# Later score products, spread-out norms and another queue for one copy, in a fused channel-attention and gated feed-forward kernel

## The chip, the cores and the metric

The kernel runs on one core of a Trainium2 chip. The metric is device time in microseconds, as the median of several runs. A core has four engines that compute and run side by side: TensorE (PE, matrix products into the PSUM memory), VectorE (DVE), ScalarE (ACT) and GpSimd (POOL). SyncE (SP) only issues transfers; GpSimd and ScalarE can issue them too. Each engine takes its instructions in program order, and semaphores make it wait for the others.

## The reference, cut to what matters

Four batches of 6016 rows and 256 channels. A channel attention makes a 256 x 256 matrix per batch from q and k, and a gated feed-forward layer follows.

```python
B, N, C = (4, 6016, 256)
qn = q / (np.linalg.norm(q, axis=1, keepdims=True) + 1e-06)
kn = k / (np.linalg.norm(k, axis=1, keepdims=True) + 1e-06)
s = kn.transpose(0, 2, 1) @ qn / tau
s = s - s.max(-1, keepdims=True)
a = np.exp(s)
a /= a.sum(-1, keepdims=True) + 1e-09
x = (v @ a).reshape(B * N, C)                       # 24064 x 256
gate = 1.0 / (1.0 + np.exp(-(x @ w_gate)))          # 256 x 1536
val = x @ w_val
out = gate * val @ w_out                            # 1536 x 256
```

## The kernel before

The kernel folds the attention matrix into the two input weights of the layer (`gh_G`, `gh_H`), so that the main loop runs on v alone. The loop goes over 4 batches, 12 chunks of 512 rows in each, and 12 blocks f of 128 hidden columns in each chunk: 144 turns per batch. Such a turn is called a slot here. In each slot TensorE makes a gate and a value tile, ScalarE the gate's function, VectorE their product hT, and TensorE about 7 output products of an earlier chunk (which are saved by a Strassen-like scheme of 7 products in place of 8, with sums of operands made on VectorE):

```python
def glu(b, ci, f, between=None):
    ...
    for ps, w in ((ps_gate, G), (ps_val, H)):
        for ib in range(CB):
            mm(ps[:, :n], w[...], vT[:, ib, :nt, :], start=(ib == 0), stop=(ib == CB - 1))
    ...
    nc.scalar.activation(out=g_sb[:, :n], in_=ps_gate[:, :n], func=ACT.Tanh, scale=0.5)
    nc.vector.scalar_tensor_tensor(out=hts[b, ci][:, f, :n], in0=g_sb[:, :n], scalar=1.0,
                                   in1=ps_val[:, :n], op0=ALU.add, op1=ALU.mult)
```

Beside this, the loop over batch b carries the statistics of batch n = b + 1 as side work, each piece tied to a slot by `at(slot, function, ...)`. Within a slot the order is: `glu`, the output products and their sums, then the side work in the order in which it was listed. q and k come in six groups of 8 row tiles (the last has 7), loaded from GpSimd's queue:

```python
def load_qk(b, t0, nt):
    tl = qkpool.tile([P, 2, 2 * TPC, C], BF16, tag="qk", name="qk_sb")      # 4 buffers
    ...
    for w, src in enumerate((q, k)):
        for u0, r0, n in parts:
            nc.gpsimd.dma_start(out=tl[:, w, u0 : u0 + n, :], in_=rows(src, b)[:, r0 : r0 + n, :])
```

The scores q^T k use 7 products in place of 8, too. Their operand sums qs0 to qs4 are made per group, qs1 by a copy and an accumulating transfer:

```python
def score_sums(b, t0, m, halves):
    ...
    out = qspool.tile([P, 2 * TPC, P], BF16, tag=f"qs{m}", name=f"qs{m}", bufs=1 + (m == 1))
    if m == 0:      # qs0: k's halves, a difference
        tt(out=o[:, :n], in0=tl[:, 1, hi, :], in1=tl[:, 1, lo, :], op=ALU.subtract)
    elif m == 1:    # qs1: q's lower half, copied
        nc.sync.dma_start(out=o[:, :n], in_=tl[:, 0, lo, :])
    ...             # qs2 of q and k, qs3 of q, qs4 of k: nc.vector.tensor_tensor

def score_sum_q(b, t0, halves):     # qs1 += q's upper half
    nc.gpsimd.dma_start(out=o[:, :n], in_=qk[b, t0][:, 0, TPC : TPC + n, :], accum_op=ALU.add)

products = (                        # of score_work; u runs over 4 tiles: 28 products in a full group
    (0, 0, raw(0, 0, 0), split(0, 1), None),        # split(m, .) and block(m, .) read qs<m>
    (0, 1, raw(0, 1, 1), split(0, 0), (...)),
    (1, 0, block(2, 0), block(2, 1), (...)),
    (1, 1, block(3, 1), block(4, 1), (...)),        # index 12 is the first of these
    (1, 2, block(3, 0), block(4, 0), None),
    (0, 2, split(1, 1), raw(1, 0, 0), None),        # index 20
    (0, 3, split(1, 0), raw(1, 1, 1), (...)),
)

def run_scores(lo, hi, slot):
    for _ in range(len(score_queue) // (hi - slot)):
        _, fn, a = score_queue.pop(0)
        fn(*a)
```

The norms: ScalarE squares q and k, GpSimd adds the squares into an accumulator by transfers, VectorE folds it, TensorE sums over the partitions, and GpSimd takes the root in 13 small operations. A row of the result goes through DRAM to all partitions.

```python
def acc_fold(b, w, steps):
    for n in steps:
        nc.vector.tensor_tensor(out=acc[:, :n, :], in0=acc[:, :n, :], in1=acc[:, n : 2 * n, :], op=ALU.add)

def norms_mm(b):                    # four products with a column of ones: two on q, then two on k
    for w in range(2):
        for j in range(CB):
            mm(s["n"][...], s["acc"][w][:, 0, ds(j * P, P)], ones_bf[:, 0:1], ...)
```

The plan of the side work stands in the diff below. In the first batch a group has 13 or 14 slots (80 slots from slot 16 on), in the second and third 16 slots (96 from slot 0 on); the fourth batch prepares nothing.

Of the kernel before, what the change touches and what calls it, by code (L numbers as in the profile page):

```python
# [53 lines left out]
def kernel(  # L54
# [20 lines left out]
    nc = tc.nc  # L75
# [21 lines left out]
    def rows(x, b):  # L97
        return x[b].rearrange("(p t) c -> p t c", p=P)
# [35 lines left out]
    def load_qk(b, t0, nt):  # L134

        tl = qkpool.tile([P, 2, 2 * TPC, C], BF16, tag="qk", name="qk_sb")
        if b and nt < 2 * TPC:

            parts = [(0, t0, nt - TPC), (TPC, t0 + nt - TPC, TPC)]
        else:  # L140
            parts = [(0, t0, nt)]
        for w, src in enumerate((q, k)):
            for u0, r0, n in parts:
                nc.gpsimd.dma_start(out=tl[:, w, u0 : u0 + n, :], in_=rows(src, b)[:, r0 : r0 + n, :])
        if b:
            qk[b, t0] = tl
            return
        for u in range(0, nt, TPC):
            qk[b, t0 + u] = [tl[:, w, u : u + TPC, :] for w in range(2)]
# [10 lines left out]
    t0, nt = groups0[0]  # L160
# [6 lines left out]
    pairs = [(t, 2 * TPC) for t in range(TPC, head - 3 * TPC, 2 * TPC)]  # L167
    loads0 = pairs + [(t, n) for t, n in groups0 if t >= pairs[-1][0] + 2 * TPC]
    load_qk(0, *loads0[0])

    ident_bf = consts.tile([P, P], BF16)
# [20 lines left out]
    for t0, nt in loads0[1:]:  # L192
        load_qk(0, t0, nt)
# [6 lines left out]
    for f0, nf in pieces:  # L200
        if f0 + nf == DFF:
            load_v(0, 1)
        for w, src in enumerate((moe_w_gate, moe_w_val)):
            nc.gpsimd.dma_start(
                out=w_sb[w][f0 // FG][:, :, ds(f0 % FG, nf)],
                in_=src.rearrange("(t p) f -> p t f", p=P)[:, :, ds(f0, nf)],
# [5 lines left out]
    for n in range(FC // TPC):  # L212
        w_f32[n] = f32pool.tile([P, TPC, C], FP32, tag="f32", name="w_f32")
        nc.gpsimd.dma_start(
            out=w_f32[n], in_=moe_w_out.rearrange("(t p) c -> p t c", p=P)[:, n * TPC : (n + 1) * TPC, :]
# [99 lines left out]
    def score_sums(b, t0, m, halves):  # L315
        tl = qk[b, t0]
        s = st[b]
        if m == 0:
            s["sums"] = []
        out = qspool.tile([P, 2 * TPC, P], BF16, tag=f"qs{m}", name=f"qs{m}", bufs=1 + (m == 1))  # L320
        s["sums"].append(out)
        n = halves[0][1]
        lo, hi = (slice(h * TPC, h * TPC + n) for h in range(2))
        tt = nc.vector.tensor_tensor
        if m == 0:

            o = out.rearrange("p (t c) n -> p t c n", c=2).rearrange("p t c n -> p t (c n)")
            tt(out=o[:, :n], in0=tl[:, 1, hi, :], in1=tl[:, 1, lo, :], op=ALU.subtract)
        elif m == 1:

            o = out.rearrange("p (t c) n -> p t c n", c=2).rearrange("p t c n -> p t (c n)")
            nc.sync.dma_start(out=o[:, :n], in_=tl[:, 0, lo, :])
        elif m == 2:

            o = out.rearrange("p (w t) n -> p w t n", w=2)
            tt(out=o[:, :, :n], in0=tl[:, :, lo, :P], in1=tl[:, :, hi, P:], op=ALU.add)
        else:

            w, op = ((0, ALU.subtract), (1, ALU.add))[m - 3]
            for u0, r in [(0, 2 * TPC)] if n == TPC else halves:  # L340
                tt(out=out[:, u0 : u0 + r], in0=tl[:, w, u0 : u0 + r, :P], in1=tl[:, w, u0 : u0 + r, P:], op=op)  # L341
# [494 lines left out]
    for g, (t0, nt) in enumerate(groups0):  # L836
# [11 lines left out]
        while adds:  # L848
            w, last_sq = adds.pop()
# [27 lines left out]
    late = []  # L877
# [27 lines left out]
    def side_work(b):  # L905


        side = {}

        def at(slot, fn, *a):  # L910
            side.setdefault(divmod(slot, FC), []).append((fn, a))

        for ci in range(NCH):
            nb, nci = (b, ci + 1) if ci + 1 < NCH else (b + 1, 0)
            lb, lci = (b, ci + 2) if ci + 2 < NCH else (b + 1, ci + 2 - NCH)
            if nb < B:
                at(ci * FC + 2, transpose_v, nb, nci)
            if lb < B:
                at(ci * FC + (10 if (b, ci) == (0, 0) else 0), load_v, lb, lci)
            if (b, ci) == (0, 0):  # L920
                for i in range(FC // TPC):
                    at(8, copy_w_out, i)
                for n, m in enumerate((1, 0, 3, 2, 4)):
                    for i in range(FC // TPC):
                        at(11 + 2 * n, sum_w_out, m, i)
        n = b + 1
        if n == B:
            return side
        first, last = (16 if b == 0 else 0), 8 * FC
        wide = [(t, min(2 * TPC, NT - t)) for t in range(0, NT, 2 * TPC)]  # L930
        step = (last - first) / len(wide)
        at(first - 1 if b == 0 else 0, acc_start, n)
        for g, (t0, nt) in enumerate(wide):
            s0 = first + int(g * step)
            halves = [(0, nt - TPC), (TPC, TPC)]
            if b == 0:
                at(max(FC - 3, s0 - 14), load_qk, n, t0, nt)
            elif s0 >= 24:
                at(s0 - 24, load_qk, n, t0, nt)
            for i in range(4):  # L940
                at(s0 + 3 * i, acc_square, n, t0, i // 2, halves, i % 2)
            for w in range(2):
                at(s0 + 5 + 6 * w, acc_add, n, t0, w, halves)
            for m, slot in enumerate((0, 0, 3, 6, 9)):
                at(s0 + slot, score_sums, n, t0, m, halves)
            at(s0 + 4, score_sum_q, n, t0, halves)
            at(s0 + 3, queue_scores, n, t0, halves)
            for slot in range(s0 + 3, first + int((g + 1) * step) + 3):
                at(slot, run_scores, s0 + 3, first + int((g + 1) * step) + 3, slot)
        if n + 1 < B:  # L950
            for g, (t0, nt) in enumerate(wide[:2]):
                at(NCH * FC - 24 + 16 * g, load_qk, n + 1, t0, nt)
        s0 = 8 * FC + 2
        at(s0 - 1, acc_fold, n, 0, (4,))
        at(s0, acc_fold, n, 0, (2, 1))
        at(s0 + 1, acc_fold, n, 1, (4,))
        at(s0 + 2, acc_fold, n, 1, (2, 1))
        at(s0 + 3, norms_mm, n)
        at(s0 + 4, root_seed, n)
        at(s0 + 4, root_steps, n)  # L960
        at(s0 + 4, score_out, n, 0)
        at(s0 + 6, score_out, n, 1)
        at(s0 + 7, score_blocks, n)
        at(s0 + 10, norms_inv, n)
        at(s0 + 11, spread_both, n)
        at(s0 + 13, read_row, n)
        at(s0 + 22, scale_x, n, 0)
        at(s0 + 24, scale_x, n, 1)
        at(s0 + 25, exps, n, 0)
        at(s0 + 26, exps, n, 1)  # L970
        at(s0 + 28, all_sums, n)
        at(s0 + 28, gh_tiles, n)
        for i, piece in enumerate(gh_order):
            slot = s0 + 29 + 2 * i
            if slot < NCH * FC:
                at(slot, gh, n, piece, *((pss, "s"), (psm, "m"))[i % 2])
            else:
                spill.setdefault((n, *divmod(slot - NCH * FC, FC)), []).append((gh, (n, piece, psm, "m")))
        return side
# [12 lines left out]
    for b in range(B):  # L992
        side = side_work(b)
        for ci in range(NCH):
            final = (b, ci) == (B - 1, NCH - 1)
            for f in range(FC):
                mid = gh_mid.get(f) if (b, ci) == (0, 0) else None
                glu(b, ci, f, None if mid is None else (lambda: gh_pieces(mid)))
                if prev is not None:
                    if f == 4:  # L1000
                        store()
                    if f + final in NEXT_SLOTS and prev != (0, 0):
                        a_sum(*prev, 1, NEXT_SLOTS[f + final])
                    run_work(work, 1 / max(1, FC - final - f))
                if f in OWN_SLOTS and not final and (b, ci) != (0, 0):
                    a_sum(b, ci, 0, OWN_SLOTS[f])
                for fn, a in spill.get((b, ci, f), []) + side.get((ci, f), []):
                    fn(*a)
                if (b, ci) == (0, 0):
                    gh_pieces(gh_end.get(f, ()))  # L1010
            prev = (b, ci)
            if not final:
                work = out_work(*prev)
# [39 lines left out]
```

## Time and profile before

| | |
|---|---|
| time, median of 3 runs | 818.26 us (817.01 to 819.18) |
| profiled span | 817.8 us |
| VectorE busy | 719.2 us, 88% |
| ScalarE busy | 525.7 us, 64% |
| GpSimd busy | 405.9 us, 50% |
| granted TensorE clock, mean | 0.994 |
| start of slot 0 of the four batches | 36.7, 244.7, 438.4, 632.2 us |
| start of slots 16 and 96 of the first batch | 56.8 and 180.7 us |
| transfers: software queue, hardware queue | 41.4% and 22.2% of 16 engines' span |

The profile gives each engine's busy time, and for each instruction how long its engine stood idle before it and what ended that. "PE ps_s <- DVE qs" is a wait of TensorE, before a product into the tile ps_s, that ended when VectorE had written qs. A line of such a list ends in the sum in us, the number of waits and the longest. In the groups, "L341" is a line of the kernel; most matmuls share line 129, a helper, so one goes by the names of tiles. The granted clock is the share of its full clock that TensorE was given. The slot starts above are read from the timeline, from the gate products.

The transfers by their issuing engine (name, engine, count, KB each, median us from issue to landing):

```profile
qk_sb<-in_q_dram POOLq DMA_DIRECT2D x19, 512.0 KB, 7.9
qk_sb<-in_k_dram POOLq DMA_DIRECT2D x19, 512.0 KB, 10.3
qs<-qk_sb SPq DMA_DIRECT2D x15, 256.0 KB, 6.4
qs<-qk_sb POOLq DMA_DIRECT2D x15, 256.0 KB, 4.0
```

### The profile page before, as it was taken

Reading aid. Unit: us, or ns where it says so; the run is one execution under the profiler, and the core shown is the slowest. Engines: PE = TensorE matmul, PEld = TensorE weight load, DVE = VectorE, ACT = ScalarE, POOL = GpSimd, SP = SyncE. Lnnn points to the kernel's source line nnn. Section 1 sums busy time; section 2 is a strip of 40 time slices with the busy share of each in tenths; the row PEclk is TensorE's granted clock in tenths of the full one; section 3 lists DMA queues with packets and bytes.
Section 4 is the critical chain, followed back from the end, with each engine's and each line's share of the span. In section 5 each row is a group of like instructions: output and inputs, shape, how many; then the busy total and the mean of one; then the engine's idle time right before and its main releaser. Section 6 shows DMA issues by size and latency. Waiting matters only on the chain.

```text
span 817.8 us, 18442 instructions
## 1 busy us (share of the span) xinstructions
PE 782.0 (96%) x6932; PEld 499.8 (61%) x6946; DVE 719.2 (88%) x1234; ACT 525.7 (64%) x893; POOL 405.9 (50%) x622
## 2 busy tenths in 40 slices
PE   3899988899999999999999999999999999999998
PEld 2555655565666666665666666666566566666666
DVE  5778978899988999999998999999998898899896
ACT  3766756665667777775666767766566566656654
POOL 3573544565543555554844355556654234444433
PEclk9999999999999999999999999999999999999999
DMA  9999889772677699865378599976142332432402
GB/s 213 204 195 175 175 166 182 146 134 52 132 140 137 134 187 182 181 131 99 52 136 152 108 181 208 185 140 125 35 104 53 84 66 53 91 65 54 93 30 71
DMA packets 85594, 103.30 MB, mean 126 GB/s; under 512 B 52737, under 2 KB 59521, under 8 KB 85505
## 3 DMA queue, kind: packets, MB, share of 16 engines
q0 software_dynamic: 25840, 59.46, 41.4%
q1 hardware_dynamic: 59088, 41.82, 22.2%
q8 instruction: 54, 0.88, 0.4%
q10 hardware_dynamic: 576, 0.85, 0.3%
q14 instruction: 36, 0.29, 0.1%
HBM read 79.04 MB, written 24.64 MB: 127 GB/s over the span
## 4 chain that ended last, share of the span: by engine, by line
PE 90%; DVE 4%; DMA 4%; issue 1%; ACT 1%; POOL 0%; DVEq 0%; POOLq 0%
PE ps_gate L129 29%; PE ps_val L129 29%; PE ps_o L129 26%; DMA qk_sb<-in_k_dram 4%; PE ps_s L129 4%; PE ps_gh L129 2%; DVE hT L657 1%; DVE sums L679 1%; DVE acc L311 1%; ACT g_sb L656 1%; DVE qs L341 1%; PE ps_end L129 0%; DVE x_sb L518 0%; PE ps_n L129 0%; PE ps_r L129 0%
## 5 line engine op out<-in xcount | busy, mean ns | idle before, releaser
L656 ACT ACTIVATE g_sb<-ps_gate 128x512 f32<-128x512 f32 (+1 forms) x576 | 337.5, 588 | 243.0 <-PE ps_gate L129 231.0
L657 DVE SCALAR_TENSOR_TENSOR hT<-g_sb,ps_val 128x512 bf16<-128x512 f32 (+1 forms) x576 | 386.1, 671 | 80.0 <-ACT g_sb L656 62.3
L129 PE MATMUL ps_gate<-vT,gh_G 128*128 128x512 bf16 (+1 forms) x1152 | 339.2, 376 | 0.4 <-ACT out_sb L764 0.3
L129 PE MATMUL ps_val<-vT,gh_H 128*128 128x512 bf16 (+1 forms) x1152 | 339.0, 376 | 0.0
L679 DVE TENSOR_TENSOR sums<-hT 128x768 bf16<-128x768 bf16 (+1 forms) x460 | 282.7, 615 | 0.0
L129 PEld LDWEIGHTS <-sums 128*128 128x128 bf16 x2670 | 183.7, 98 | 82.5 <-issue 0.8
L129 PEld LDWEIGHTS <-gh_H 128*128 128x128 bf16 x1152 | 112.9, 98 | 131.7 <-issue 2.0
L750 POOL TENSOR_TENSOR out_sb<-out_sb,m_sb 128x256 f32<-128x256 f32 x89 | 79.5, 893 | 206.2 <-ACT out_sb L740 178.0
L129 PE MATMUL ps_o<-w_sums,sums 128*128 128x128 bf16 x1602 | 155.4, 220 | 0.0
L129 PEld LDWEIGHTS <-hT 128*128 128x128 bf16 x1200 | 88.3, 98 | 47.2 <-issue 0.6
L734 POOL TENSOR_TENSOR m_sb<-m_sb 128x128 f32<-128x128 f32 x89 | 44.8, 503 | 138.2 <-ACT m_sb L733 138.0
L129 PEld LDWEIGHTS <-gh_G 128*128 128x128 bf16 x1152 | 90.8, 98 | 11.6 <-DMA vT<-v_sb 0.5
L129 PE MATMUL ps_o<-w_out_sb,sums 128*128 128x128 bf16 x1068 | 96.4, 220 | 0.0
L129 PE MATMUL ps_o<-w_sums,hT 128*128 128x128 bf16 x1068 | 95.8, 220 | 0.0
L751 POOL TENSOR_TENSOR out_sb<-out_sb 128x256 f32<-128x256 f32 x89 | 76.6, 861 | 7.0
L293 ACT ACTIVATE sq<-qk_sb 128x1024 bf16<-128x1024 bf16 (+1 forms) x60 | 61.9, 1031 | 0.0
L740 ACT COPY out_sb<-ps_o 128x512 f32<-128x512 f32 x89 | 52.1, 586 | 11.2 <-PE ps_o L129 8.8
L735 POOL TENSOR_TENSOR m_sb<-m_sb 128x128 f32<-128x128 f32 x89 | 54.4, 611 | 7.0
L733 ACT COPY m_sb<-ps_o 128x384 f32<-128x384 f32 x89 | 42.5, 478 | 3.8 <-PE ps_o L129 1.1
L129 PEld LDWEIGHTS <-qk_sb 128*128 128x128 bf16 x241 | 23.6, 105 | 21.1 <-issue 10.0
L304 POOL DMA_DIRECT2D acc<-sq x36 | 34.9, 1028 | 0.8 <-ACT g_sb L656 0.5
L129 PEld LDWEIGHTS <-qs 128*128 128x128 bf16 x348 | 27.3, 99 | 10.3 <-issue 10.3
(98 smaller groups left out, 462.5 us busy)
## 6 DMA issues: line engine op xcount, KB each, us to landing
out_dram<-out_sb SPq DMA_DIRECT2D x43, 512.0 KB, 3.4
acc<-sq POOLq DMA_DIRECT2D x24, 512.0 KB, 6.9
v_sb<-in_v_dram POOLq DMA_DIRECT2D x44, 256.0 KB, 5.6
qk_sb<-in_q_dram POOLq DMA_DIRECT2D x19, 512.0 KB, 7.9
qk_sb<-in_k_dram POOLq DMA_DIRECT2D x19, 512.0 KB, 10.3
qs<-qk_sb SPq DMA_DIRECT2D x15, 256.0 KB, 6.4
qs<-qk_sb POOLq DMA_DIRECT2D x15, 256.0 KB, 4.0
w_f<-in_moe_w_out_dram POOLq DMA_DIRECT2D x3, 512.0 KB, 9.9
```

The costliest lines, as they stand in the source:

```text
L129: nc.tensor.matmul(out, lhsT=lhsT, rhs=rhs, start=start, stop=stop, **kw)
L293: nc.scalar.activation(out=s["sq", w][:, u0 : u0 + n, :], in_=src[:, u0 : u0 + n, :], func=ACT.Square)
L304: nc.gpsimd.dma_start(out=s["acc"][w][:, u0 : u0 + n, :], in_=s["sq", w][:, u0 : u0 + n, :], accum_op=ALU.add)
L656: nc.scalar.activation(out=g_sb[:, :n], in_=ps_gate[:, :n], func=ACT.Tanh, scale=0.5)
L657: nc.vector.scalar_tensor_tensor(out=hts[b, ci][:, f, :n], in0=g_sb[:, :n], scalar=1.0, in1=ps_val[:, :n], op0=ALU.add, op1=ALU.mult,)
L679: nc.vector.tensor_tensor(out=sums[b, ci, g][:, m, :, : half * P], in0=hT[:, f0 + k0 : f1 : 2, ds(r0 * half * P, half * P)], in1=hT[:, f0 ...
L733: nc.scalar.copy(m, states[p]["ps"][:, : 3 * P].rearrange("p (n c) -> p n c", c=P))
L734: nc.gpsimd.tensor_tensor(out=m[:, 1, :], in0=m[:, 1, :], in1=m[:, 2, :], op=ALU.add)
L735: nc.gpsimd.tensor_tensor(out=m[:, 2, :], in0=m[:, 1, :], in1=m[:, 0, :], op=ALU.add)
L740: nc.scalar.copy(o[:, p : p + half + 1 : half, :], states[p]["ps"].rearrange("p (t c) -> p t c", c=C),)
L750: add(out=ends, in0=ends, in1=states[p]["m"][:, 1:3, :], op=ALU.add)
L751: add(out=ends, in0=ends, in1=mids, op=ALU.subtract)
```

## The change

It moves side work to other slots and changes no arithmetic. In the first batch, the score products of a group begin five slots after the group's start instead of three, and qs4 is made one slot earlier. The squares, folds and loads of k come before those of q. The folds, the norm products, the root and the row are spread over more slots, with the norm products later, and the blocks of the score matrix are put together after the row is sent. The copy of q into qs1 is issued by GpSimd instead of SyncE, one slot later, and the accumulation onto it two slots later. It is meant to give each operand more time between its making and its reading, so that TensorE need not stand for it.

```diff
-        for w, src in enumerate((q, k)):
+        for w, src in ((1, k), (0, q)) if b else ((0, q), (1, k)):
             for u0, r0, n in parts:
                 nc.gpsimd.dma_start(out=tl[:, w, u0 : u0 + n, :], in_=rows(src, b)[:, r0 : r0 + n, :])
 ...
-            nc.sync.dma_start(out=o[:, :n], in_=tl[:, 0, lo, :])
+            nc.gpsimd.dma_start(out=o[:, :n], in_=tl[:, 0, lo, :])
 ...
             for i in range(4):
-                at(s0 + 3 * i, acc_square, n, t0, i // 2, halves, i % 2)
+                at(s0 + 3 * i, acc_square, n, t0, 1 - i // 2, halves, i % 2)
             for w in range(2):
-                at(s0 + 5 + 6 * w, acc_add, n, t0, w, halves)
-            for m, slot in enumerate((0, 0, 3, 6, 9)):
+                at(s0 + 11 - 6 * w, acc_add, n, t0, w, halves)
+            late = 5 if b == 0 else 3
+            for m, slot in enumerate((0, 1, 3, 6, 8 if b == 0 else 9)):
                 at(s0 + slot, score_sums, n, t0, m, halves)
-            at(s0 + 4, score_sum_q, n, t0, halves)
-            at(s0 + 3, queue_scores, n, t0, halves)
-            for slot in range(s0 + 3, first + int((g + 1) * step) + 3):
-                at(slot, run_scores, s0 + 3, first + int((g + 1) * step) + 3, slot)
+            at(s0 + 6, score_sum_q, n, t0, halves)
+            end = first + int((g + 1) * step) + late
+            at(s0 + late, queue_scores, n, t0, halves)
+            for slot in range(s0 + late, end):
+                at(slot, run_scores, s0 + late, end, slot)
 ...
         s0 = 8 * FC + 2
-        at(s0 - 1, acc_fold, n, 0, (4,))
-        at(s0, acc_fold, n, 0, (2, 1))
-        at(s0 + 1, acc_fold, n, 1, (4,))
-        at(s0 + 2, acc_fold, n, 1, (2, 1))
-        at(s0 + 3, norms_mm, n)
-        at(s0 + 4, root_seed, n)
-        at(s0 + 4, root_steps, n)
-        at(s0 + 4, score_out, n, 0)
-        at(s0 + 6, score_out, n, 1)
-        at(s0 + 7, score_blocks, n)
-        at(s0 + 10, norms_inv, n)
-        at(s0 + 11, spread_both, n)
-        at(s0 + 13, read_row, n)
+        at(s0 - 3, acc_fold, n, 1, (4,))
+        at(s0 - 2, acc_fold, n, 1, (2, 1))
+        at(s0 + 1 if b == 0 else s0, acc_fold, n, 0, (4,))
+        at(s0 + 2, acc_fold, n, 0, (2, 1))
+        at(s0 + 5, score_out, n, 0)
+        at(s0 + 6, norms_mm, n)
+        at(s0 + 7, score_out, n, 1)
+        at(s0 + 7, root_seed, n)
+        at(s0 + 7, root_steps, n)
+        at(s0 + 12, norms_inv, n)
+        at(s0 + 12, spread_both, n)
+        at(s0 + 14, read_row, n)
+        at(s0 + 14, score_blocks, n)
         at(s0 + 22, scale_x, n, 0)
```

## The prediction

> **What bounds the kernel now.** I read the page's busy table and its chain first, then the waits of TensorE, then the chain around one wait, then the stretches in a table. A "slot" is one f step of the main loop; batch b of the main loop carries, as side work, the attention statistics of batch b + 1.
>
> ```profile
> PE 782.0 (96%) x6932; PEld 499.8 (61%) x6946; DVE 719.2 (88%) x1234; ACT 525.7 (64%) x893; POOL 405.9 (50%) x622
> PE 90%; DVE 4%; DMA 4%; issue 1%; ACT 1%; POOL 0%; DVEq 0%; POOLq 0%
> ```
>
> TensorE is the bound: 96% busy, 90% of the chain that ended last. A change that touches no matmul can only win back the time in which TensorE stands, or runs at less than its clock. So the question is where it stands. The waits of TensorE after the head (window from 40 us to the end):
>
> ```profile
> PE ps_s L129 <- DVE qs L341: 9.6, 6, 2.2
> PE ps_s L129 <- DVE acc L311: 5.4, 3, 1.8
> PE ps_gate L129 <- ACT out_sb L764: 0.3, 1, 0.3
> ```
>
> Ten waits, 15.3 us, and every large one is in the code that the diff moves. The six on qs all lie between 70 and 177 us, in the loop's first batch; the three on acc come once per batch that prepares another. One of the six, in the chain of waits (start, us, what):
>
> ```profile
> 108.65 0.45 PE ps_gate L129 x2
> 109.10 0.02 issue
> 109.12 0.60 ACT g_sb L656
> 109.73 0.02 issue
> 109.75 0.69 DVE hT L657
> 110.44 0.76 DVE sums L679
> 111.20 0.87 DVE qs L341
> 112.07 0.04 issue
> 112.12 0.27 PE ps_s L129 x2
> ```
>
> This is no overload of VectorE but a loop through three engines: the sum qs4 is put into the same slot (s0+9) as the first product that reads it. VectorE is in order, so qs4 stands behind that slot's hT, which waits for ScalarE, which waits for that slot's gate product. TensorE gets to the end of the slot and must wait for the whole round trip, 2.2 us here.
>
> The stretches (window, PE, PEld, DVE, ACT, POOL busy, granted clock, DMA share, GB/s):
>
> ```profile
> 57.00:181.00 124.00, 114.13 (x1017) 73.44 (x1016) 104.76 (x171) 81.15 (x131) 64.52 (x90) 0.97 0.86 165
> 112.40:115.90 3.50, 3.50 (x16) 1.81 (x15) 1.16 (x2) 0.75 (x2) 0.00 (x0) 0.51 0.63 118
> 181.00:191.00 10.00, 8.19 (x78) 5.19 (x76) 9.04 (x17) 4.81 (x9) 4.48 (x7) 1.00 0.64 133
> 245.00:353.00 108.00, 107.95 (x990) 69.34 (x990) 99.86 (x168) 77.64 (x128) 55.23 (x80) 1.00 0.86 166
> ```
>
> The first stretch is the first batch's score work: TensorE idle for 9.87 of 124 us and the clock at 0.97. The second lies just after the wait above: the clock is 0.51. The fourth is the same work in the second batch, with nothing lost: there a group has 16 slots instead of 13.3, so the product that reads qs4 falls one slot later, and that one slot is enough.
>
> **What the Trainium skill says.** "TensorE: Matmul & The Clock Gate", section "Part 1: The HAM clock gate (the "warmup" mystery)", puts TensorE at half clock after an idle window of about 3.4 us and back at full clock after as long a busy one. The trace agrees on the half and on the way back: after the 2.2 us wait the 128x512 matmuls start about 427 ns apart instead of 216 until 115.9 us, and again near 136 to 139 us. It differs on what it takes: waits of 2.2 us were enough here, though not each time (not after the one that begins near 154.7 us), and after the two shorter ones nothing shows. So a wait can cost more than its own length. "DMA: Bandwidth & Descriptors", section "Queues, rings and completion order", says that each queue keeps its own ring per DMA engine, that descriptors of one ring are taken in order, and that the engine goes round the rings. The trace agrees: a qs accumulation issued by GpSimd at 102.63 us, behind the q and k loads issued at 97.58 and 98.17, landed at 110.02, after k's 108.67. The same page, "Issuing engines are not separate DMA queues", says that another issuing engine saves only issue time. Here the copies on SyncE took 5.2 to 7.5 us to land beside such loads, so the same bytes will not get cheaper by moving; what changes is which line they stand in.
>
> **The change part by part.**
>
> 1. Score products two slots later in the first batch, and qs4 one slot earlier. 28 products of a full group go over 13 or 14 slots, two per slot, so the first reader of qs4 (product index 12) moves from slot s0+9 to s0+5+6 = s0+11, and qs4 from s0+9 to s0+8. The distance goes from 0 to 3 slots, 3 x 1.37 = 4.1 us. The longest wait is 2.2 us, and in the second batch one slot (1.35 us) is enough. All six waits go: 9.9 us of idle time in 57 to 181 us.
> 2. With them the low clock: 0.03 x 124 = 3.7 us. A second count: slot 16 of the first batch starts at 56.8 us and slot 96 at 180.7 us, 123.9 us for 80 slots. The second batch runs at 1.352 us per slot with 165 score products in 96 slots; the same 165 in 80 slots add (2.06 - 1.72) x 56 ns = 0.02 us, so 80 x 1.371 = 109.7 us, and the excess is 14.2 us, of which some 0.5 us is the first chunk's dearer plain output products. 13.6 and 13.7 us agree.
> 3. Norms. The second accumulator's fold now ends at s0-2 (k) and s0+2 (q), and the norm products come at s0+6 instead of s0+3: four slots after the last fold instead of one. The four folds (0.69, 0.75, 0.94 and 1.13 us in the trace) no longer stand in four slots running. 3 x 1.8 = 5.4 us.
> 4. k before q: the same bytes. k's squares, folds and differences come first, so its earlier landing (10.5 us against 7.3 for the one issued first) is what part 3 needs. By itself 0.
> 5. The copy of q from GpSimd: 18 issues of 0.9 us (measured for the qs accumulation), 16 us more on an engine that is 50% busy, not on the path.
>
> Sum: 13.6 + 5.4 = 19.0 us; 818.26 - 19.0 = 799.3 us. I add 1 us for what follows, and predict **800.3 us**.
>
> **Rivals.** *The copy becomes the wait.* SyncE ran far ahead: it issued the fourth group's copy at 107.4 us, 12 us before that group's first slot (119.4). GpSimd goes in step with the loop, and in the first batch the next group's loads stand just ahead in its ring (slots 28, 42, 55, 68 against copies at 30, 43, 57, 70). Landing may take 10 to 12 us from the loads' issue; GpSimd then stands at the accumulation (slot s0+6) for 2 to 4 us, as it does once today (5.8 us), and the sum lands 5 to 8 us later, about slot s0+13 to s0+14. Its first reader (product index 20) is at the end of slot s0+15. By my working 1 to 5 us are left; if it fails in each of five groups by 1 to 2 us, the time is 805 to 809 us. For it speaks that the 16 DMA engines are 86% busy there and the same work will be pressed into 110 us, 97%; against it, that between 280 and 320 us they are as full and nothing waits.
>
> *VectorE becomes the bound of the first batch.* It is busy for 104.8 us there, of some 110 left, 95%. In the second batch it is at 99.9 of 108, 92%, and from 353 to 374 us it is busy for 20.8 of 21.0 us without a wait of TensorE, whose gate and value tiles have two buffers each. I give it 0 to 2 us: 800 to 802.
>
> *GpSimd's root is late.* The root's 13 small operations take 4.8 us (193.4 to 198.2); root_seed to norms_inv is now 5 slots of 1.254 us = 6.3 us, before it was 6. If GpSimd is still at an output addition, VectorE stands, in order, up to 1 us in each of three batches: at most 802. The row itself has more room: score_blocks (3.7 us) now stands behind the row's issue instead of ahead of it, and today the row is issued only at 205.75 us.
>
> *The waits are moved, not removed* (TensorE meets the next late thing): then 815 to 818 us. Against it speaks the second batch, where the same chain runs with no idle time at all.
>
> **Range and chances.** The floor is the full 19.6 us or so that the count of slots allows, 798.6, and a little below by the spread of the runs (817.0 to 819.2); the copy rival makes the upper end. Range 797.5 to 805.5. Two per cent faster is 801.9 us, only 1.6 us above my figure: 0.69 for faster by over 2%, 0.29 for within, 0.02 for slower, as nothing here adds work to TensorE.
>
> **What would show it.** Right: no wait of ps_s on qs or acc is left; the granted clock is 1.00 between 57 and 170 us; slots 16 to 96 of the first batch take about 110 us; GpSimd some 16 us busier. Wrong: a wait of ps_s on a DMA into qs (the copy), waits of ps_val or ps_gate on hT (VectorE), a wait of r_wide on GpSimd (the root), or a first batch that stays above 115 us with another releaser.

## Result, and the profile after

| | us |
|---|---|
| before, median of 4 runs on the same chip | 817.63 (816.76 to 819.18) |
| after, median of 4 runs | 805.24 (804.08 to 806.67) |
| ratio | 0.9847, 95% interval 0.9824 to 0.987 |
| predicted | 800.3, range 797.5 to 805.5 |

The change saves 12.4 us, 1.5%: inside the range but near its upper end, and short of the 2% to which I had given 0.69.

From the page of the changed kernel, the busy table and the shares of the chain that ended last:

```profile
PE 777.9 (97%) x6932; PEld 497.6 (62%) x6946; DVE 717.9 (89%) x1234; ACT 525.2 (65%) x893; POOL 416.1 (52%) x640
PE 89%; DMA 8%; DVE 1%; issue 1%; POOL 1%; ACT 0%; DVEq 0%; ACTq 0%; POOLq 0%
```

VectorE's share of the chain fell from 4% to 1%, and that of transfers rose from 4% to 8%. The waits of TensorE from 40 us to the end say what replaced what:

```profile
PE ps_s L129 <- DMA qs<-qk_sb: 2.0, 1, 2.0
PE ps_gate L129 <- DMA vT<-v_sb: 0.8, 1, 0.8
PE ps_val L129 <- DVE hT L657: 0.7, 2, 0.5
```

All nine large waits of before (six on qs, three on acc) are gone: 15.0 us became 3.5 us in four waits. But the first line is a wait on a transfer into qs, the sign that the prediction gave for the copy as the new wait.

The first batch's score work, six microseconds within it, and the same work in the second batch (window, PE, PEld, DVE, ACT, POOL busy, granted clock, DMA share, GB/s):

```profile
57.00:170.00 113.00, 109.96 (x1010) 71.03 (x1009) 103.33 (x170) 80.17 (x130) 68.40 (x96) 1.00 0.99 180
118.00:124.00 6.00, 6.00 (x63) 4.03 (x61) 5.87 (x11) 5.01 (x9) 3.58 (x4) 1.00 0.97 40
233.00:341.00 108.00, 107.95 (x985) 69.11 (x985) 99.89 (x168) 77.84 (x128) 57.82 (x85) 1.00 0.87 169
```

The clock is full, and the second batch is as it was. The middle line is odd: the 16 DMA engines are 97% busy and move 40 GB/s, where the whole stretch has 180. The transfers issued between 105 and 132 us, in which those six microseconds fall (last number: us from issue to landing):

```profile
qk_sb<-in_k_dram POOLq DMA_DIRECT2D x1, 512.0 KB, 13.9
qk_sb<-in_q_dram POOLq DMA_DIRECT2D x1, 512.0 KB, 17.8
vT<-v_sb SPq DMA_TRANSPOSE x1, 13.8
```

Before, the loads of the same group took 7.9 (q) and 9.3 us (k), and the transpose of v beside them 3.1 us. GpSimd in order of time shows what that does (start, us, line, what; in brackets idle time before):

```profile
112.38 0.83 POOL L144 DMA_DIRECT2D qk_sb<-in_k_dram  x1
112.92 0.84 POOL L144 DMA_DIRECT2D qk_sb<-in_q_dram  x1
116.98 0.58 POOL L332 DMA_DIRECT2D qs<-qk_sb  x1
...
121.87 0.91 POOL L304 DMA_DIRECT2D acc<-sq  x1
132.32 0.87 POOL L346 DMA_DIRECT2D qs<-qk_sb  x1 [9.55 <-DMA qs<-qk_sb]
```

The copy (L332) was issued at 116.98 us behind the two loads and landed at 131.77. GpSimd stood at the accumulation (L346), which needs the copy, for 9.55 us, and TensorE then for 2.0 us, from 134.8 us on. A transfer of ScalarE's squares (L304), issued ahead of that wait, took 13.5 us itself, and it is this one, not the copy, that the chain that ended last goes through (start, us, what):

```profile
121.87 13.53 DMA acc<-sq
...
136.39 0.59 ACT g_sb L656
136.97 0.03 issue
137.00 0.70 DVE hT L657
137.70 0.04 issue
137.74 0.59 PE ps_val L129 x2
```

Between the first two lines ScalarE had stood 3.5 us for that transfer before its next squares, so the gate's function (L656) came late, then hT, then the next value tile. Two late transfers thus hold the loop at the same moment, and by this chain the copy alone on time would not have freed TensorE.

To see where the time went I cut three profiled executions at the gate products; slots have the names of the prediction. The last column is the changed kernel with the copy back on SyncE (an experiment below).

| us | before | after | after, copy on SyncE |
|---|---|---|---|
| start to slot 16 of the first batch | 56.8 | 56.9 | 56.9 |
| its slots 16 to 96 (scores) | 123.9 | 113.2 | 110.5 |
| slots 96 to 110 (norms), three batches | 19.95, 19.95, 19.95 | 18.89, 17.99, 17.99 | 18.90, 17.99, 17.99 |
| slot 138 of the last batch to the end | 13.2 | 14.1 | 13.2 |
| span | 817.8 | 803.1 | 799.5 |

Everything between these pieces is equal to 0.1 us. So the whole result lies in three places: 10.7 us won in the scores, 5.0 in the norms, and 0.9 lost at the very end, where the change touches nothing.

### The profile page after: what moved, and what is told of

Its sections match the earlier page's. It is cut to its first block, busy times and chain, and to the rows that moved or that the text cites. A ratio compares the mean times of both kernels' runs of the same rounds, so it can differ in the third digit from the quotient of the medians.

```text
span 803.1 us, 18395 instructions
## 1 busy us (share of the span) xinstructions
PE 777.9 (97%) x6932; PEld 497.6 (62%) x6946; DVE 717.9 (89%) x1234; ACT 525.2 (65%) x893; POOL 416.1 (52%) x640
## 4 chain that ended last, share of the span: by engine, by line
PE 89%; DMA 8%; DVE 1%; issue 1%; POOL 1%; ACT 0%; DVEq 0%; ACTq 0%; POOLq 0%
PE ps_gate L129 29%; PE ps_val L129 29%; PE ps_o L129 26%; DMA qk_sb<-in_k_dram 4%; PE ps_s L129 3%; PE ps_gh L129 2%; DMA acc<-sq 2%; DMA vT<-v_sb 1%; DMA v_sb<-in_v_dram 1%; DVE hT L657 0%; DVE acc L311 0%; POOL qk_sb L144 0%; PE ps_end L129 0%; ACT g_sb L656 0%; POOL out_sb L750 0%
## 5 line engine op out<-in xcount | busy, mean ns | idle before, releaser
L656 ACT ACTIVATE g_sb<-ps_gate 128x512 f32<-128x512 f32 (+1 forms) x576 | 337.3, 588 | 224.8 <-PE ps_gate L129 214.1
L734 POOL TENSOR_TENSOR m_sb<-m_sb 128x128 f32<-128x128 f32 x89 | 46.0, 517 | 124.7 <-ACT m_sb L733 124.5
L735 POOL TENSOR_TENSOR m_sb<-m_sb 128x128 f32<-128x128 f32 x89 | 55.4, 623 | 7.0
L129 PE MATMUL ps_s<-qk_sb 128*128 128x256 bf16 (+1 forms) x103 | 17.3, 317 | 15.9 <-DMA qk_sb<-in_k_dram 9.1
L346 POOL DMA_DIRECT2D qs<-qk_sb x18 | 19.4, 1077 | 25.0 <-DMA qs<-qk_sb 24.8
```

What stands on the lines that cost most here:

```text
L129: nc.tensor.matmul(out, lhsT=lhsT, rhs=rhs, start=start, stop=stop, **kw)
L734: nc.gpsimd.tensor_tensor(out=m[:, 1, :], in0=m[:, 1, :], in1=m[:, 2, :], op=ALU.add)
L735: nc.gpsimd.tensor_tensor(out=m[:, 2, :], in0=m[:, 1, :], in1=m[:, 0, :], op=ALU.add)
```

## Experiments

**The two halves alone.** My theory: the score part and the norms part add up, and what is missing is the copy. Rival: the waits of one part come back in the other. First the kernel before with only the norms part of the diff (squares, additions, folds, norm products, root and row; loads, copy and score products as before).

> The kernel before with the norms part alone (k's squares and additions before q's, folds, norm products, root, row and score blocks at the slots of the changed kernel). Theory A (three separate kinds of waits, each worth its own length): the three waits of the norm products on the folds go, 3 x 1.8 = 5.4 us, so about 812.2 us against 817.6 before; the six waits on qs stay at some 9.6 us. Rival B (the norms' waits only move to the next thing that is late): under 2 us, 816 or more, with waits of ps_val or ps_gate on hT after slot 96 in their place.

813.22 us, ratio 0.9942 (0.9926 to 0.9959), 4.8 us won. Its waits of TensorE:

```profile
PE ps_s L129 <- DVE qs L341: 9.5, 6, 2.2
PE ps_val L129 <- DVE hT L657: 0.7, 1, 0.7
```

The waits on acc are gone, those on qs untouched. The second line is new: in the first batch slots 96 to 102 gain 2.06 us, but slots 102 to 110 give back 1.0 of it (11.04 us for 10.03), where VectorE is busy for 10.5 of the 11.0 us and its hT comes late once.

Then the kernel before with only the score part, the copy staying on SyncE in slot s0:

```diff
-            for m, slot in enumerate((0, 0, 3, 6, 9)):
+            late = 5 if b == 0 else 3
+            for m, slot in enumerate((0, 0, 3, 6, 8 if b == 0 else 9)):
 ...
-            at(s0 + 3, queue_scores, n, t0, halves)
-            for slot in range(s0 + 3, first + int((g + 1) * step) + 3):
-                at(slot, run_scores, s0 + 3, first + int((g + 1) * step) + 3, slot)
+            end = first + int((g + 1) * step) + late
+            at(s0 + late, queue_scores, n, t0, halves)
+            for slot in range(s0 + late, end):
+                at(slot, run_scores, s0 + late, end, slot)
```

> The kernel before with the first batch's score products two slots later and qs4 one slot earlier, nothing else; the copy of q stays on SyncE's queue, loads stay q before k. Theory A: the six waits on qs and the half-clock stretches go, 11 to 13.6 us, so 804 to 807 us, and no wait of ps_s on a transfer appears. Rival B (VectorE is the next bound in the first batch): 6 us or less, 811 or more, with waits of ps_val on hT between 57 and 171 us.

806.21 us, ratio 0.9857 (0.9842 to 0.9872), 11.8 us won, almost all that the whole change wins. Waits:

```profile
PE ps_s L129 <- DVE acc L311: 5.2, 3, 1.8
PE ps_val L129 <- DVE hT L657: 1.0, 1, 1.0
```

No wait on qs, neither for VectorE nor for a transfer. Slots 16 to 96 took 110.5 us.

**How much of the score part is one slot?** The kernel before with nothing but qs4 at s0+8 in the first batch:

```diff
-            for m, slot in enumerate((0, 0, 3, 6, 9)):
+            for m, slot in enumerate((0, 0, 3, 6, 8 if b == 0 else 9)):
```

> The kernel before with qs4 one slot earlier in the first batch (s0+8 instead of s0+9) and nothing else: the score products stay where they were. Theory A (the wait is the round trip of one slot: gate product, gate function, hT, qs4): one slot of distance, 1.37 us and more, takes away most of it as it does in the second batch; 9 to 13 us, so 805 to 809. Rival B (the two later slots are what counts): the waits of 2.2 us shrink by one slot to about 0.9 us, gain 6 us or less, 811 or more.

809.08 us, ratio 0.9887 (0.9871 to 0.9904), 9.0 us won, at the lower edge of what theory A gave. The waits on qs that are left:

```profile
PE ps_s L129 <- DVE qs L341: 1.9, 3, 1.0
```

One slot (1.37 us) of distance takes the six waits from 9.6 us to three of 1.9 us together; the longest, once 2.2 us, is now at most 1.0. That is about what subtracting one slot from a round trip of 2.2 us leaves. The gain is larger than the 7.7 us of waiting that went, as the two stretches at half clock went too: in this profile the granted clock is 1.00 from 57 to 170 us. The second and third slot are worth another 2.9 us.

**The copy back on SyncE,** all else as in the changed kernel:

```diff
-            nc.gpsimd.dma_start(out=o[:, :n], in_=tl[:, 0, lo, :])
+            nc.sync.dma_start(out=o[:, :n], in_=tl[:, 0, lo, :])
```

> The changed kernel with the copy of q issued by SyncE again (slot and all else as changed). Theory A (the shortfall of the change comes from the copy's place behind the next loads in GpSimd's ring): the wait of ps_s on the transfer into qs (2.0 us), GpSimd's 24.8 us at the accumulation, and ScalarE's wait for a squares buffer (3.5 us) go; about 802.5 us, 2 to 3.5 below the changed kernel's 805.2. Rival B (the queue does not matter, the first batch is held by VectorE, or by transposes that collide with the loads): 804.5 to 806.

801.6 us, ratio 0.9807 (0.9788 to 0.9825), 16.5 us won, which is 11.8 + 4.8: the halves add. The only wait of TensorE left after 40 us, and the six microseconds from above:

```profile
PE ps_val L129 <- DVE hT L657: 1.5, 2, 1.0
```

```profile
118.00:124.00 6.00, 6.00 (x61) 3.95 (x58) 5.87 (x10) 5.01 (x9) 4.50 (x5) 1.00 1.09 256
```

256 GB/s instead of 40, and k and q land 8.2 and 9.9 us after issue. A second set of this same kernel, beside other ones:

> The changed kernel with the copy of q on SyncE again, a second time, beside the other two on one chip: 801.3 to 803.9 us as before, no wait of ps_s on a transfer, loads that land within 11 us.

801.5 us, ratio 0.9795 (0.975 to 0.984), no wait on the copy. The copy on GpSimd costs about 3.6 us. The kernels compared were timed on different chips; by their ratios to before it is 3.3 us with the first set and 4.3 us with the second.

**Is the jam at 118 us an accident of one profile?** The changed kernel, unchanged, again:

> The changed kernel itself, once more, for a second profile and beside the other three on one chip. If the late loads near 112 us and the 2.0 us wait belong to the schedule, they are there again and the time is 804 to 806.5 us; if they were an accident of one run, the profile shows no wait of ps_s on a transfer and the times spread more.

806.84 us, ratio 0.9844 (0.9817 to 0.9871). The same six microseconds, and its first waits:

```profile
118.00:124.00 6.00, 6.00 (x57) 3.83 (x55) 6.00 (x11) 4.76 (x8) 3.77 (x5) 1.00 1.21 50
```

```profile
PE ps_s L129 <- DMA qs<-qk_sb: 2.0, 1, 2.0
PE ps_gate L129 <- DMA vT<-v_sb: 1.6, 1, 1.6
```

It repeats: loads 14.0 and 17.9 us, transpose 13.9 us, GpSimd standing 9.6 us. It is a property of the kernel. Here the wait also brought back what the change was to remove: a stretch of 3.4 us at half clock, from 137.5 us on, as the clock of the whole stretch shows (0.98, where the first profile has 1.00):

```profile
57.00:170.00 113.00, 109.38 (x990) 70.52 (x989) 101.51 (x167) 79.23 (x129) 65.72 (x93) 0.98 0.99 178
```

**What makes the jam?** In the changed kernel the transpose of v (issued by SyncE as soon as that v has landed) starts at 112.23 us, 0.15 us ahead of k's load. Before, the same transpose started at 115.77 and the loads at 118.93. With the copy on SyncE it starts at 112.95, 0.2 us behind the second load. So I suspected the order of transpose and loads. In the first of two tests v is loaded four slots earlier, so that its transpose is done before the loads:

```diff
-                at(ci * FC + (10 if (b, ci) == (0, 0) else 0), load_v, lb, lci)
+                at(ci * FC + (10 if (b, ci) == (0, 0) else -4 if b == 0 and ci > 1 else 0), load_v, lb, lci)
```

> The changed kernel with v's loads four slots earlier in the first batch, so that the transposes of v, which start as soon as v has landed, end before the next q and k loads start (in the changed kernel's trace they start 0.05 to 0.5 us apart, and a load takes up to 17.8 us to land). Theory A1 (the shortfall is a collision of the transposes with the loads, which the faster loop brought together): the loads land in 6 to 10 us again, the wait on the transfer into qs goes, 802 to 803 us. Rival A2 (the copy stands behind the loads in GpSimd's ring and GpSimd stands at the accumulation, whatever the transposes do): 804.5 to 806, GpSimd's wait at the accumulation still 15 us or more in sum.

803.05 us, ratio 0.9803 (0.978 to 0.9827). The loads land after 7.9 and 10.1 us, 229 GB/s in the six microseconds, and TensorE waits for no transfer into qs. GpSimd still stands at the accumulation, for 18.2 us in six waits, as rival A2 had said, but no wait of TensorE on such a transfer comes of it. The second test puts 2 in place of -4, so that the transpose starts at 114.51 us, 1.3 us behind k's load:

> The changed kernel (copy on GpSimd) with v's loads two slots later in the first batch from the third chunk on, so that the transposes still run beside the q and k loads but start some 2 us after them instead of together. If what hurts is that transposes start just ahead of the loads, the loads land in 6 to 11 us, the wait on the transfer into qs goes, 802 to 804 us. If any overlap of transposes and loads does it, a load still takes over 13 us somewhere and the time is 805 or more.

```profile
118.00:124.00 6.00, 6.00 (x57) 3.80 (x55) 6.00 (x11) 4.53 (x7) 4.00 (x5) 1.00 1.05 229
```

Its longest wait:

```profile
PE ps_gate L129 <- DMA vT<-v_sb: 1.6, 1, 1.6
```

The loads land after 8.2 and 9.8 us and the jam is gone here too, so a transpose that overlaps the loads is not enough to make it. Nor is one that starts just ahead of them: in the changed kernel's own trace another transpose starts at 75.93 us, 0.05 us ahead of k's load, and those loads land after 5.9 and 8.6 us. The time, 804.77 us (0.9825, 0.9795 to 0.9856), is a little above what I had expected, and 3.3 us above the kernel with the copy on SyncE, which ran beside it on the same chip. So taking the jam away does not take the copy's cost away. This profile has a wait of 1.6 us on vT near 68 us, which the edit does not touch; that this is the rest is not shown.

**Does the copy's place in the line matter?** The copy stays on GpSimd but is issued two slots before the group, except in the first group:

```diff
+            if b == 0 and g:
+                at(s0 - 2, copy_ahead, n, t0, halves)
```

> The changed kernel with the copy of q still issued by GpSimd, but two slots before the group instead of one slot after its start, in the first batch from its second group on, so ahead of the next group's loads in the ring. Theory A2 (place in the ring): GpSimd's wait at the accumulation falls from 24.8 us to under 10, no wait of ps_s on the transfer, 801.5 to 803. Theory A1 (collision with the transposes) or anything else about GpSimd's queue: 804 to 806, and loads that land late.

804.94 us, ratio 0.9829 (0.9802 to 0.9856): a miss, I had expected 801.5 to 803. TensorE no longer waits for a transfer into qs, and GpSimd's own waits at the accumulation fall from 24.8 us in seven to 10.1 us in three. But a wait of 1.6 us on vT and three on hT, 1.1 us together, stand in the list instead. It also weakens the suspicion about order: here the transpose starts 0.06 us ahead of the copy and 0.6 us ahead of k's load, and the loads land after 9.4 and 12.3 us: later than elsewhere, but without a jam.

**The order of the loads.** The changed kernel with q ahead of k again:

```diff
-        for w, src in ((1, k), (0, q)) if b else ((0, q), (1, k)):
+        for w, src in enumerate((q, k)):
```

> The changed kernel with q loaded before k again, the only part of the change undone. Theory A2 (the copy waits in the ring behind all loads, in whichever order): no difference, 804.5 to 806. Rival C (k first is what makes the copy late, as q lands later): the wait on the transfer into qs goes, 802 to 803.

804.53 us, ratio 0.9821 (0.9796 to 0.9846). The ratio cannot be told from that of after, but on the same chip the repeat of after took 806.84 us (804.51 to 807.34, against 803.49 to 805.40 here), so a cost of k first of 1 or 2 us is not excluded. The loads are late in this one too, 12.8 and 16.6 us, behind a transpose that starts 0.12 us ahead of the first, with 0.8 us of waiting on the copy.

**Both cures at once,** the copy on SyncE and v four slots earlier:

> The changed kernel with the copy of q on SyncE again and v's loads four slots earlier in the first batch: both cures at once. If both act on the same loss (late loads and what waits for them), together they give no more than one alone: within 1.5 us of the changed kernel with SyncE's copy, which runs beside it, and 801 to 803 us. If the copy's queue and the collision are two losses, it is another 2 to 3 us below, 799 or less.

801.13 us, ratio 0.9783 (0.9753 to 0.9813), as with the copy on SyncE alone: together they win no more than the better one. A wait of 0.9 us of TensorE on a transfer into qs stands in this profile, in the third batch, so such a wait is not tied to GpSimd's queue.

**The end of the program.** With the copy on GpSimd, slot 138 of the last batch lies 14.1 us before the end in all six profiles; with it on SyncE, and before, it lies 13.2 us before the end in all seven. What differs is GpSimd's closing DRAIN instruction in the trace: 6.40 us in the six, where GpSimd issued 195 transfers, and 5.26 us in the others, where it issued 177. At 5.26 us it ends 0.3 us before SyncE reaches the closing barrier, at 6.40 us it is the last to come. To find whether the number of transfers sets it, I took the kernel with the copy on SyncE and let GpSimd issue 36 transfers of 256 bytes in the last batch, whose result nobody reads:

```diff
+    spare_sb = consts.tile([P, P], BF16)
+    def spare():
+        nc.gpsimd.dma_start(out=spare_sb[0:1, :], in_=ones_bf[0:1, :])
 ...
         if n == B:
+            for i in range(36):
+                at(8 + 3 * i, spare)
             return side
```

> The changed kernel with the copy back on SyncE, plus 36 tiny transfers (256 bytes each, read by nobody) that GpSimd issues in the last batch. In all runs so far with the copy on GpSimd (195 transfers issued by it) its closing instruction at the end of the program takes 6.40 us, and with the copy on SyncE (177 transfers) 5.26 us; the end of the span lies 14.1 us after slot 138 of the last batch in the first case and 13.2 us in the second. Theory A (the closing instruction grows with the number of transfers that GpSimd issued, 1.14/18 = 0.064 us each): with 213 transfers it takes 7.55 us, the end lies 15.2 us after slot 138, and the time is about 2.0 us above the kernel with the copy on SyncE, 803 to 804 us. Theory B (it is the bytes or packets of the copies, or something else of them): it stays at 5.26 us, 13.2 us, and 801 to 802 us.

803.88 us, ratio 0.9814 (0.9788 to 0.9839), 2.4 us more than the kernel without them. The closing DRAIN took 8.20 us. The last piece of the chain of waits, under the line that gives the span, for the copy on SyncE and for this one (start, us, what):

```profile
core 0 of [0], span 799.5 us
...
796.37 0.29 DVE end L814
```

```profile
core 0 of [0], span 802.2 us
...
796.36 0.29 DVE end L814
```

The last arithmetic of both ends at about 796.65 us; what follows takes 2.8 us in one and 5.5 us in the other, with nothing but tiny transfers, long landed, as the difference. In after it is 3.7 us. It is the count, not the bytes: 1.14 us for 18 more (64 ns each) and 2.94 us for 36 more (82 ns each), a little steeper than my 0.064 us each foresaw.

## Why the prediction was right or wrong

**Steps 1 and 2 (score products, clock): right, but measured from the wrong height.** Slots 16 to 96 fell from 123.9 to 110.5 us where the copy did not disturb them: 13.4 us for the 13.6 that I had counted. Free of waits a slot took 1.366 to 1.374 us, as I had put it. Yet the medians show 11.8 us. The profile of before that I read was of an execution of 819.72 us with a mean clock of 0.994, and I took its gain off the median, 818.26 us. Runs of before differ in this: their spans were 814.2 to 815.1 us where the granted clock was 0.998, 815.7 to 818 at 0.996, and 817.5 to 818.7 at 0.994. The profiled run, at 0.994, had two stretches at half clock in the score work, and step 2's 3.7 us was the price of both. As an estimate from these spans, the median run has about half of it. That is 1.5 us of the error, the difference between 819.72 and 818.26. Step 2 also took the full clock as won for good, and in the repeat of after a wait on the copy lost part of it again.

**Step 3 (norms): right, 5.0 us for 5.4.** The second and third batch gave 1.96 us each, more than the 1.8 I took; the first gave 1.06. There the VectorE rival came true for a moment: slots 102 to 110 became 0.8 us longer, with TensorE waiting 0.5 us for hT.

**Step 4 (k first, 0):** not contradicted, and not shown; the kernel with q first leaves room for a cost of 1 or 2 us.

**Step 5 (the copy, "not on the path") failed.** I counted issue time on an idle engine, and even that was less than I took: an issue takes 0.58 us, GpSimd is 10 us busier, not 16. The cost lies elsewhere. Between the spans 803.1 and 799.5 it is 2.6 us in slots 69 to 82 (20.43 for 17.87 us), 0.9 at the end, and 0.2 elsewhere. In the repeat of after the first of these is 3.9 us, with the stretch at half clock in it. The 0.9 at the end is GpSimd's longer closing instruction, which no rival had named.

The first part has the sign of the rival *the copy becomes the wait*, and its steps (loads ahead in the ring, GpSimd standing at the accumulation, the sum too late), but not its size or its whole path. I had loads of 10 to 12 us and five groups short by 1 to 2 us each. In fact four of the five groups after the first had room, and one met a jam of 14 to 18 us that nothing in my working foresaw. The jam held everything in GpSimd's line, the squares' transfer with the copy, and the chain that ended last runs through the squares. "Issuing engines are not separate DMA queues" in the Trainium skill's "DMA: Bandwidth & Descriptors" says that starting transfers from several engines saves only the time of issuing them; here no such saving is seen, and the move to another engine cost 3.6 us.

Why the jam arises is not settled. Shown is that it repeats, that it goes when v is loaded four slots earlier or when its transpose starts 1.3 us behind k's load, and that it is absent with the copy on SyncE, where the transpose starts behind k's load too. In the three profiles that have it (after, its repeat, q first) the transpose starts 0.12 to 0.15 us ahead of the first load. But 0.05 us ahead, at 75.93 us in after, does no such thing, and neither does 0.6 us with a copy between, so this order is at most a part of it. Why the 16 engines move only 40 to 77 GB/s there, no run tells.

Nor is the jam all of the cost, as the kernel with v two slots later shows. A further piece may lie near 68 us, where TensorE waits 0.6 to 1.6 us for vT in every kernel with the copy on GpSimd and at most 0.5 us in those with the copy on SyncE. Slot 29 starts at 75.6 to 76.7 us in the six profiles, on average 76.2, and at 74.5 to 76.0 us, on average 75.4, in the five that have the late score products and the copy on SyncE. The ranges overlap and no run tests it, so the 0.8 us is a guess at its size, which I leave out of the sum.

**The other rivals.** No wait for GpSimd's root appeared. *The waits are moved, not removed* is wrong for the score and norms parts, as their halves show.

**The sum.** 800.3 us was 818.26 - 19.0 + 1. Taking 1.5 for the height, 3.6 for the copy and 0.6 for the sizes of steps 1 to 3 (18.4 for 19.0), and giving back the allowance of 1 us, makes 805.0 us; measured were 805.2. The medians of single sets are not that exact (the four runs of after go from 804.1 to 806.7 us, and its repeat has 806.8), so the close agreement is partly luck. So is the place inside the range: its upper end was set by the copy's rival, but the height and the end of the program, 2.4 us together, stood nowhere in the working. The chance of 0.69 was too high because it rested on a figure 1.6 us under the line, with step 5 set at zero and the reading of one execution taken as typical.

The best version is the changed kernel with the copy on SyncE: 801.6 and 801.5 us in two sets, about 2% under before. Loading v earlier as well (801.1 us) makes no difference that can be told.

## What to carry to other kernels

An operand made in the slot of its first reader costs a whole round trip through the other engines, and here one slot of distance took back 9.0 of 11.8 us, three slots all of it; look for such pairs before counting busy time. Before moving a transfer to another engine, list what stands ahead of it and behind it in that engine's line, what else starts in the same microsecond, and how long the engine's closing instruction already is. And take a gain off the time of the execution whose profile it was read from, not off the median.

## What the runs showed of the hardware that I had not expected

- GpSimd's closing DRAIN grew with the number of transfers that it had issued: 5.26 us for 177, 6.40 us for 195, 8.20 us for 213, the last 36 of them 256 bytes each. Where it ends after the other engines, it is time.
- The DMA engines were 97% busy in six microseconds and moved 40 GB/s (121% and 50 GB/s in the repeat), where the changed kernel's variants without the jam moved 213 to 256 in the same stretch. The share counts how long packets stay open. Of the 97%, 95 belong to GpSimd's queue, with 57 packets, 1.6 us each on average; with the copy on SyncE that queue had 216 packets of 0.28 us. Busy share alone doesn't tell work from a jam; the rate beside it does.
- Half clock followed a wait of TensorE of 2.0 to 2.2 us in some places and not in others. In before it followed the waits that ended at 112.1 and 135.2 us and not that of 157.0 us; in the changed kernel the wait of 2.0 us on the copy brought none in one profile and 3.4 us in the other. So the gain of removing such a wait depends on the run; the times of before spread from 816.2 to 820.4 us in one set of seven.
